# Two buffers for the layer's turned input, and an earlier place for its transposes

## The chip, the cores and the metric

One core of a Trainium2 chip runs the whole program. The metric is the device time of one execution in microseconds (us); lower is better. A kernel's time is the median of its runs.

## The reference, cut to what matters

```
def _attn_ref(q, k, v, beta):            # B=4, H=8, S=768, D=48, float32
    k_n = k / (norm(k) + 1e-06)
    for t in range(S):
        y[:, :, t] = q[:, :, t] @ state
        v_old = state^T k_n[:, :, t]
        state = state + beta_t * outer(k_n[:, :, t], v_t - v_old)

def _moe_ref(x, w_in, w_out):            # 3072 tokens, 384 -> 2048 -> 384
    h = x @ w_in
    sp = log1p(exp(min(h, 20)))  (h itself above 20)
    return (h * tanh(sp)) @ w_out
```

`reference` computes the first, lays its y out as 3072 rows of 384 (token by head and depth), and puts them through the second. The first part is a recurrence over 768 steps for 32 pairs of batch and head; the second is a layer with one weight matrix in and one out.

## The kernel before, in words

The sequence is cut into `NS` = 12 chunks of `C` = 64 steps. For each chunk n the recurrence is turned into matrix products: products of keys, a triangular solve (`early`, one for two chunks, a long chain of VectorE steps in L296 and L301, ended by the transposes of L308 and L317), and the stages `s_a`, `s_b`, `s_gq`, `s_z` and `s_y`, which are small matmuls with a copy by ScalarE or VectorE behind each. `s_y(n, h)` gives the output y of the chunk for half h of the pairs: ScalarE copies it into the tile `yy` (L487), and the state for the next chunk into `xx` (L486).

The layer works on the 256 tokens of a chunk. `transposed(n, y)` turns y (called a turn here): six TensorE transposes (L505) into two PSUM tiles `xt`, two ScalarE casts to the high part of x (L507), two VectorE subtractions to its low part (L508). The transposes of the first 128 tokens need half 0 of y, the others half 1. `g1(fp)`, for 8 units fp of 256 hidden columns each, runs 18 first-layer matmuls (L530) into a PSUM tile `h`, of which there are two, and then the activation: L534 (ScalarE), L535 (VectorE), L536, L537, L538 (ScalarE), L539 (VectorE, which reads `h` last and frees it), L549 (ScalarE), L552 (VectorE). `g2(fp)` runs 12 second-layer matmuls (L564) on the result; it is issued two units behind `g1`.

In which order all this is traced is written down as due times in chunks: `put(gen, count, t0, t1)` files steps of a generator between t0 and t1, and the plan is run in order of those times. With NFP = 8, `g1(fp)` of chunk n is due at n + (fp + 0.25)/8 and a `g2` at n + (fp + 0.75)/8. `s_y(n, 1)`, which completes y of chunk n, is due at n - 0.2 from chunk 3 on (at 0.6 for n = 1, at 1.8 for n = 2); the stage `s_a` of an even chunk just behind it at n - 1.19, and `s_b` with the next `s_a` at n - 1.07 (n even), so both fall to the boundary ahead of an odd chunk. The turn of chunk n (L708 to L710) is due at n - 0.5/8. A solve for two chunks (L737) runs from 2.6 chunks ahead of its even chunk to 1.5 ahead.

A planner with a time model then settles each engine's order from these priorities and from when inputs are ready. On TensorE that freedom ends for what is due at 0.9 (`m0`) or later: its instructions are issued there in the order of the due times (L744 to L748). ScalarE and VectorE keep the planner's order all along. Each engine executes its order as laid down, and each instruction waits for its inputs.

Pools: `mp` has a tile of its own for each tag and buffer; `x0` and `x1` (high and low part of x) have `bufs=1`, so the turn of chunk n writes them after the last `g1` of chunk n - 1 has read them. The PSUM pool `pa` (tag `at`, four buffers) serves `xt` and nearly all matmuls of the stages.

Around a boundary into chunk n, TensorE's order before the change is thus: g1(n-1,6); s_y(n,1); [s_a at odd n]; a g2; g1(n-1,7); [s_b and s_a at odd n]; the turn of n; a g2; g1(n,0).

Of the kernel before, what the change touches and what calls it, by code (L numbers as in the profile page):

```python
# [10 lines left out]
F32R = mybir.dt.float32r  # L11
# [23 lines left out]
def kernel(  # L35
# [32 lines left out]
    P = 128  # L68
# [4 lines left out]
    NCH = DM // P  # L73
    NF = DFF // P
    NFP = NF // 2
    UT = B * C
# [8 lines left out]
    mp = ctx.enter_context(tc.tile_pool(name="mp", bufs=2))  # L85
# [412 lines left out]


    def transposed(n, y):  # L500
        xs = [mp.tile([P, NCH, UT], F32R, tag=f"x{i}", name=f"x{i}_{n}", bufs=1) for i in range(2)]
        for t in range(UT // P):
            ps = pa.tile([P, NCH, P], F32, tag="at", name=f"xt{n}_{t}")
            for c in range(NCH):
                nc.tensor.transpose(ps[:, c, :], y[:, t, c * P:(c + 1) * P], ident)  # L505
            hi = xs[0][:, :, t * P:(t + 1) * P]
            nc.scalar.copy(out=hi, in_=ps)  # L507
            nc.vector.tensor_tensor(out=xs[1][:, :, t * P:(t + 1) * P], in0=ps, in1=hi, op=ALU.subtract)  # L508
        return xs
# [83 lines left out]
    ys, xs = {}, {}  # L593

    def turn(n):
        if n < NS:
            xs[n] = transposed(n, ys[n])

    def one(f, *a):
        f(*a)  # L600
        yield
# [3 lines left out]
    def put(gen, n, t0, t1):  # L605
        plan.extend((t0 + (t1 - t0) * (i + 0.5) / n, len(plan), gen) for i in range(n))
# [72 lines left out]
    for i, p in enumerate(parts):  # L679
        ny = 4 if i >= TN.get('sg', 14) else 3  # L680
        for j in range(ny):
            x = i + (j + 0.5) / ny
            for (t0, i0), (t1, i1) in zip(cuts, cuts[1:]):
                if i0 <= x < i1:
                    t = t0 + (t1 - t0) * (x - i0) / (i1 - i0)
# [8 lines left out]
    t = 0.0  # L694
    lag = 2
    for k, (n, fp) in enumerate(todo1):
        t = n + (fp + 0.25) / NFP
# [3 lines left out]
        elif k >= lag:  # L701
            m, fq = todo2.pop(0)
            t = n + (fp + 0.75) / NFP
# [2 lines left out]
        put(one(units[m][1], fq), 1, NS + i, NS + i)  # L706
    put(merge(1), 4, *TN['m1'])
    for n in range(1, NS):  # L708
        t = n - 0.5 / NFP
        put(one(turn, n), 1, t, t)  # L710

        t = TN['p1'] if n == 1 else TN['p2'] if n == 2 else n - 1.85
        put(one(prep, n), 1, t, t)
# [11 lines left out]
    for g in range(1, NS // 2):  # L725
        n = 2 * g
# [58 lines left out]
```

## Time and profile before

| | |
|---|---|
| median of 3 runs | 746.64 us (746.27 to 752.27) |
| profiled execution, own time | 750.13 us |
| its span, first to last instruction | 748.4 us |
| mean granted TensorE clock, as a share of 2.4 GHz | 0.905 |

The profile is of one execution. Its page gives each engine's busy time and a strip of 40 slices; the trace behind it gives each instruction's start and duration, what its engine waited for, and the clock granted to TensorE in any stretch. The engines are written PE (TensorE), PEld (its weight loads), DVE (VectorE), ACT (ScalarE), POOL (GpSimd) and SP (SyncE). An idle time in brackets behind a row is the time for which that engine stood before the instruction, and behind the arrow is what ended it.

### The profile page before, as it was taken

Reading aid. Unit: us, or ns where it says so; the run is one execution under the profiler, and the core shown is the slowest. Engines: PE = TensorE matmul, PEld = TensorE weight load, DVE = VectorE, ACT = ScalarE, POOL = GpSimd, SP = SyncE. Lnnn points to the kernel's source line nnn. Section 1 sums busy time; section 2 is a strip of 40 time slices with the busy share of each in tenths; the row PEclk is TensorE's granted clock in tenths of the full one; section 3 lists DMA queues with packets and bytes.
Section 4 is the critical chain, followed back from the end, with each engine's and each line's share of the span. In section 5 each row is a group of like instructions: output and inputs, shape, how many; then the busy total and the mean of one; then the engine's idle time right before and its main releaser. Section 6 shows DMA issues by size and latency. Waiting matters only on the chain.

```text
span 748.4 us, 22288 instructions
## 1 busy us (share of the span) xinstructions
PE 638.7 (85%) x9653; PEld 590.4 (79%) x9670; DVE 509.8 (68%) x1011; ACT 432.0 (58%) x793; POOL 136.2 (18%) x171
## 2 busy tenths in 40 slices
PE   5667455793998899898998997998998989999993
PEld 3236344793897799797998997998997989999993
DVE  4788999757459975389963698864799735553441
ACT  2224534563555567565666646675655777776771
POOL 5343243772032224000010010010000100000000
PEclk9757665796999899899999998999999999999997
DMA  5858710110341222122212302311112121000000
GB/s 83 196 173 243 224 24 1 22 24 1 44 80 30 33 55 45 28 50 31 43 36 35 63 14 33 66 30 26 34 24 34 42 33 34 12 9 15 6 18 21
DMA packets 160210, 37.72 MB, mean 50 GB/s; under 512 B 153456, under 2 KB 156528, under 8 KB 160112
## 3 DMA queue, kind: packets, MB, share of 16 engines
q1 hardware_dynamic: 160112, 36.30, 23.7%
q8 instruction: 76, 1.25, 0.7%
q14 instruction: 22, 0.18, 0.1%
HBM read 31.56 MB, written 4.72 MB: 48 GB/s over the span
## 4 chain that ended last, share of the span: by engine, by line
PE 47%; DVE 26%; ACT 8%; POOL 5%; SPq 5%; issue 5%; DMA 3%; DVEq 0%; POOLq 0%; ACTq 0%
PE h L530 20%; PE acc L564 17%; SPq L137 5%; DVE gt L301 5%; DVE pr L296 4%; PE gq L395 3%; DVE e L539 2%; PE py L395 2%; DMA vt<-in_v_dram 1%; DVE e L535 1%; DVE gt L252 1%; POOL gt L301 1%; PE pz L395 1%; ACT e L536 1%; POOL pr L296 1%
## 5 line engine op out<-in xcount | busy, mean ns | idle before, releaser
L530 PE MATMUL h<-x,wi 128*128 128x256 f32 x1728 | 239.1, 294 | 27.8 <-ACT x L507 15.3
L530 PEld LDWEIGHTS h<-x,wi 128*128 128x128 f32 x1728 | 229.6, 200 | 35.1 <-ACT x L507 17.9
L564 PE MATMUL acc<-wo,g 128*128 128x384 f32 x1152 | 222.8, 342 | 0.1
L564 PEld LDWEIGHTS acc<-wo,g 128*128 128x128 f32 x1152 | 198.2, 188 | 3.8 <-issue 0.2
L539 DVE SCALAR_TENSOR_TENSOR e<-e,h 128x512 f32<-128x512 f32 x96 | 65.6, 684 | 89.5 <-ACT e L538 89.0
L536 ACT ACTIVATE e<-e 128x512 f32<-128x512 f32 x96 | 60.6, 631 | 60.7 <-DVE e L535 60.6
L534 ACT ACTIVATE e<-h 128x512 f32<-128x512 f32 x96 | 57.1, 595 | 66.4 <-PE h L530 61.0
L535 DVE TENSOR_SCALAR e<-e 128x512 f32<-128x512 f32 x96 | 44.4, 463 | 69.6 <-ACT e L534 69.5
L549 ACT CAST g<-e 128x512 fp32r<-128x512 f32 x96 | 59.4, 619 | 54.2 <-DVE e L539 53.8
L376 POOL TENSOR_TENSOR vt<-vt,ne 128x384 f32<-128x384 f32 x24 | 21.7, 905 | 238.3 <-DVE ne L286 109.0
L538 ACT ACTIVATE e<-e 128x512 f32<-128x512 f32 x96 | 60.6, 632 | 2.5
L537 ACT ACTIVATE e<-e 128x512 f32<-128x512 f32 x96 | 60.6, 631 | 2.5
L552 DVE TENSOR_TENSOR g<-e,g 128x512 fp32r<-128x512 f32 x72 | 49.8, 692 | 15.6 <-ACT g L549 14.0
L296 DVE TENSOR_TENSOR pr<-gt 128x228 f32<-128x228 f32 (+14 forms) x147 | 55.2, 376 | 5.1 <-POOL gt L301 1.1
L301 DVE TENSOR_TENSOR gt<-gt,pr 128x228 f32<-128x228 f32 (+14 forms) x147 | 52.9, 360 | 3.3
L395 PE MATMUL gq<-xx,kt 64*64 64x112 f32 (+1 forms) x768 | 49.6, 288 | 0.6 <-ACT at L247 0.6
L395 PE MATMUL py<-xx 128*64 128x48 f32 x768 | 43.9, 230 | 7.2 <-ACT xx L464 7.2
L395 PEld LDWEIGHTS py<-xx 128*64 128x64 f32 x768 | 40.1, 143 | 11.6 <-ACT xx L464 8.7
L552 POOL TENSOR_TENSOR g<-e,g 128x512 fp32r<-128x512 f32 x24 | 31.8, 1325 | 75.7 <-ACT g L549 48.9
L395 PEld LDWEIGHTS gq<-xx,kt 64*64 64x64 f32 x768 | 43.7, 156 | 1.5 <-ACT at L247 0.9
L395 PE MATMUL pz<-vt,tt 64*64 64x48 f32 x768 | 40.8, 245 | 3.9 <-DVE vt L443 3.9
L395 PEld LDWEIGHTS pz<-vt,tt 64*64 64x64 f32 x768 | 36.8, 148 | 8.7 <-issue 6.1
(98 smaller groups left out, 782.7 us busy)
## 6 DMA issues: line engine op xcount, KB each, us to landing
ri<-in_moe_w_in_dram SPq DMA_DIRECT2D x12, 512.0 KB
ro<-in_moe_w_out_dram SPq DMA_DIRECT2D x16, 384.0 KB
vt<-in_v_dram SPq DMA_DIRECT2D x48, 96.0 KB
xx<-in_k_dram SPq DMA_DIRECT2D x48, 96.0 KB
out_dram<-o SPq DMA_DIRECT2D x24, 192.0 KB
qsrc<-in_q_dram SPq DMA_DIRECT2D x48, 64.0 KB
ksrc<-in_k_dram SPq DMA_DIRECT2D x44, 64.0 KB
qsrc<-in_q_dram SPq DMA_DIRECT2D x48, 32.0 KB
```

Of the source, the lines that this page charges most:

```text
L296: queue(eng.tensor_tensor(out=pv, in0=nj, in1=xj, op=ALU.mult), on)
L301: queue(eng.tensor_tensor(out=below, in0=below, in1=pv, op=ALU.add), on)
L395: last[:] = [nc.tensor.matmul(*a, start=True, stop=True)]
L530: nc.tensor.matmul(h[:, f2, :], wt["i", f * P // WI * NCH + c][:, i2, f0:f0 + P], x[:, c, :], start=(i == 0), stop=(i == 3 * NCH - 1))
L534: nc.scalar.activation(e, h, AF.Exp)
L536: nc.scalar.activation(e, e, AF.Square)
L537: nc.scalar.activation(e, e, AF.Ln, bias=0.5, scale=0.5)
L538: nc.scalar.activation(e, e, AF.Exp, scale=-1.0)
L539: nc.vector.scalar_tensor_tensor(e, e, -1.0, h, op0=ALU.add, op1=ALU.mult)
L549: nc.scalar.copy(out=gg[:, 0], in_=e)
L552: eng.tensor_tensor(out=gg[:, 1], in0=e, in1=gg[:, 0], op=ALU.subtract)
L564: nc.tensor.matmul(acc[t], gg[:, a, f2, ts_], wt["o", f][:, i2, :], start=(f == 0 and i == 0), stop=(f == NF - 1 and i == 2))
```

## The change

The two parts of x get two buffers each. The turn of chunk n, for n from 1 on, is due at n - 1.1/8: behind the g2 that is due at n - 1.25/8 and ahead of g1(n-1,7), due at n - 0.75/8. For n = 1 that is 0.8625.

```diff
     def transposed(n, y):
-        xs = [mp.tile([P, NCH, UT], F32R, tag=f"x{i}", name=f"x{i}_{n}", bufs=1) for i in range(2)]
+        xs = [mp.tile([P, NCH, UT], F32R, tag=f"x{i}", name=f"x{i}_{n}", bufs=2) for i in range(2)]
...
     for n in range(1, NS):
-        t = n - 0.5 / NFP
+        t = n - 1.1 / NFP
         put(one(turn, n), 1, t, t)
```

## Rows read from the trace of the kernel before

**Rows 1.** The page: busy time of each engine with its share of the span; the granted TensorE clock in 40 slices of the span, in tenths; and the shares of the engines in the chain of work that ended last.
```profile
PE 638.7 (85%) x9653; PEld 590.4 (79%) x9670; DVE 509.8 (68%) x1011; ACT 432.0 (58%) x793; POOL 136.2 (18%) x171
...
PEclk9757665796999899899999998999999999999997
...
PE 47%; DVE 26%; ACT 8%; POOL 5%; SPq 5%; issue 5%; DMA 3%; DVEq 0%; POOLq 0%; ACTq 0%
```

**Rows 2.** Waits of TensorE's matmuls from 190 us to the end: waiter, what it waited for, total us, how often, the longest.
```profile
PE h L530 <- ACT x L507: 15.3, 8, 2.8
PE h L530 <- DVE x L508: 7.3, 7, 2.3
PE h L530 <- DVE e L539: 5.0, 5, 1.8
PE pg L241 <- DVE kt L222: 1.3, 1, 1.3
PE pg L241 <- issue: 1.2, 2, 0.6
```

**Rows 3.** TensorE's timeline, rows of L530 that had to wait: start, duration, instruction and count, idle time ahead of it. First one that lies outside a turn, then those of turns 3, 5 and 9.
```profile
232.52 2.37 PE L530 MATMUL h<-x,wi 128*128 128x256 f32 x18 [0.81 <-DVE e L539]
...
303.05 4.67 PE L530 MATMUL h<-x,wi 128*128 128x256 f32 x18 [2.80 <-ACT x L507]
...
406.98 0.38 PE L530 MATMUL h<-x,wi 128*128 128x256 f32 x1 [2.17 <-ACT x L507]
407.65 3.19 PE L530 MATMUL h<-x,wi 128*128 128x256 f32 x17 [0.29 <-DVE x L508]
...
614.44 0.38 PE L530 MATMUL h<-x,wi 128*128 128x256 f32 x1 [2.14 <-ACT x L507]
615.11 2.28 PE L530 MATMUL h<-x,wi 128*128 128x256 f32 x17 [0.29 <-DVE x L508]
```

**Rows 4.** Stretches behind the stalls of turns 2 (two), 3, 4, 5, 6, 7, 8 and 9: length, busy time and count of each engine, then the mean granted clock as a share of 2.4 GHz, the DMA engines' share and GB/s.
```profile
238.00:246.00 8.00, 6.19 (x35) 5.87 (x34) 7.63 (x16) 6.11 (x11) 1.45 (x1) 0.79 0.24 42
246.00:256.00 10.00, 6.34 (x61) 5.70 (x63) 9.24 (x19) 4.93 (x9) 2.92 (x2) 0.83 0.31 39
302.00:312.00 10.00, 8.86 (x91) 8.20 (x92) 3.91 (x10) 5.06 (x11) 1.27 (x1) 0.66 0.01 3
354.00:363.00 9.00, 7.05 (x89) 6.49 (x90) 7.94 (x21) 5.98 (x12) 0.00 (x0) 0.81 0.17 21
406.00:414.00 8.00, 6.73 (x87) 6.17 (x88) 3.48 (x9) 3.98 (x9) 0.00 (x0) 0.79 0.01 2
458.00:468.00 10.00, 7.81 (x86) 7.25 (x87) 8.01 (x23) 5.76 (x12) 0.00 (x0) 0.66 0.16 21
512.00:520.00 8.00, 7.26 (x90) 6.69 (x91) 4.13 (x10) 4.24 (x9) 0.00 (x0) 0.79 0.01 2
563.00:571.00 8.00, 5.52 (x80) 5.19 (x82) 6.87 (x19) 4.47 (x9) 0.00 (x0) 0.79 0.23 28
612.00:620.00 8.00, 5.57 (x89) 4.79 (x88) 3.48 (x8) 4.87 (x10) 0.00 (x0) 1.00 0.01 3
```

**Rows 5.** Timelines of TensorE and ScalarE at even turns: the second-layer group behind which the turn comes to stand and the copy of y's second half, at turns 2 and 8 (the first and the last of four), and at turn 4 the ScalarE instruction ahead of the copy that waited for VectorE.
```profile
236.61 2.38 PE L564 MATMUL acc<-wo,g 128*128 128x384 f32 x12
243.07 0.46 ACT L487 COPY yy<-py 128x384 f32<-128x384 f32 x1
...
344.72 0.64 ACT L536 ACTIVATE e<-e 128x512 f32<-128x512 f32 x1 [4.57 <-DVE e L535]
...
553.79 2.38 PE L564 MATMUL acc<-wo,g 128*128 128x384 f32 x12
559.39 0.46 ACT L487 COPY yy<-py 128x384 f32<-128x384 f32 x1
```

**Rows 6.** Timelines of ScalarE, TensorE and VectorE at turn 3: the copy of y's second half, the group ahead of the new place, g1(2,7), the turn's transposes, the next second-layer group, the turn's casts and subtractions.
```profile
290.52 0.48 ACT L487 COPY yy<-py 128x384 f32<-128x384 f32 x1 [0.72 <-PE ps L395]
291.60 2.38 PE L564 MATMUL acc<-wo,g 128*128 128x384 f32 x12
293.81 2.30 PE L530 MATMUL h<-x,wi 128*128 128x256 f32 x18
...
297.26 0.87 PE L505 MATMUL xt<-ident,yy 128*128 128x128 f32 x6
297.89 2.36 PE L564 MATMUL acc<-wo,g 128*128 128x384 f32 x12
302.13 0.86 ACT L507 CAST x<-xt 128x384 fp32r<-128x384 f32 x2
302.64 1.02 DVE L508 TENSOR_TENSOR x<-xt,x 128x384 fp32r<-128x384 f32 x2 [2.06 <-ACT x L507]
```

**Rows 7.** Timelines of TensorE and VectorE at turn 1: the wait for the solve, the turn's transposes, its first subtraction, and the wait for the transpose of the next keys.
```profile
181.33 1.92 PE L395 MATMUL ta<-tt,at 32*32 32x32 f32 x64 [10.90 <-DVE tt L308]
...
190.33 0.82 PE L505 MATMUL xt<-ident,yy 128*128 128x128 f32 x6
191.58 0.55 DVE L508 TENSOR_TENSOR x<-xt,x 128x384 fp32r<-128x384 f32 x1
...
194.58 1.99 PE L241 MATMUL pg<-kt 64*32 64x64 f32 x128 [1.32 <-DVE kt L222]
```

## The prediction

> **What bounds the kernel now.** I read the page first: TensorE is busy 85% of the span, VectorE 68%, ScalarE 58%; the chain that ended last runs 47% over TensorE and 26% over VectorE, and the line of the granted clock has dips between the nines [rows 1]. The first quarter is start-up, on which the change bears only in turn 1. So I asked for TensorE's waits from 190 us on. There are five rows, and two of them are this change's subject: the first-layer matmuls `h` wait 15.3 us for the cast of x (L507) and 7.3 us for its low part (L508), 22.6 us of 30.1; 5.0 us are waits for the buffer of `h` that L539 frees, the rest 2.5 us [rows 2]. Outside these TensorE never idles there, so a microsecond taken from a stall comes off the end unless something else is late next.
>
> Then the timeline at each chunk boundary. Turns 2 to 9 stall, 10 and 11 don't. They are of two kinds. At odd turns (3, 5, 7, 9) one wait of 2.14 to 2.80 us for the cast is followed by one of 0.29 us for the low part [rows 3]. At even turns (2, 4, 6, 8) VectorE is full, 7.94 us busy of 9 at turn 4 [rows 4], with the next triangular solve, and what it owes the layer comes late: ScalarE sits 4.57 us for L535 before it can go on, and in its order the copy of y stands behind that [rows 5].
>
> The fourth view is the granted clock. After most of these stalls it is at half, that is 1.2 instead of 2.4 GHz, for some microseconds: 0.66 on average over 302 to 312 us, 0.79 over 406 to 414, 1.00 over 612 to 620, where the stall was about as long [rows 3, 4]. That time is in no list of waits.
>
> **Part by part.** *The two buffers.* They add no instruction. They remove the write-after-read of x, so that a turn may run before the old chunk's last `h` has read x. Without the move TensorE's hand-written order would hide that; with it, this is what lets the transposes go ahead. The six transposes, two casts and two subtractions of a turn are the same as before: 0.87 us of TensorE at turn 3 [rows 6], and no DMA is among them, so SyncE's and GpSimd's queues lose and gain nothing.
>
> *The move.* A turn's transposes are now issued behind the second-layer group ahead of g1(n-1,7), and not behind g1(n-1,7) itself. Until g1(n,0) needs x there are 18 matmuls of 2.30 us and a second-layer group of 2.36 us in between [rows 6], at odd turns s_b and s_a too. Cast and subtraction took 0.86 and 1.02 us [rows 6]. So x is ready if the cast is not held back over some 3 us.
>
> A. Odd turns, stalls. y is there: at turn 3 its copy ends at 290.52 + 0.48 = 291.00, the group before the new place ends at 291.60 + 2.38 = 293.98 [rows 6]. So no wait for y, and the wait for x goes: 2.80 + (2.17 + 0.29) + (2.17 + 0.29) + (2.14 + 0.29) = 10.15 us (turns 3, 5, 7 and 9; turn 7's two rows read as turn 5's do) [rows 3].
>
> B. Odd turns, clock. A window of length L with mean clock c, with TensorE working in it, loses about (1 - c) L: 3.4 + 1.68 + 1.68 + 0 = 6.76 us [rows 4]. With no stall I count all of it as regained. Its ends are 0 and 6.8.
>
> C. Even turns, stalls. The x waits go there too: 22.6 - 10.15 = 12.45 us. But now TensorE meets the transposes before y is copied, and g1(n-1,7) stands queued behind them. The group before them ends at 238.99, 347.13, 450.78 and 556.17; the copy of y at 243.53, 350.26, 454.56 and 559.85 (four turns, the first and the last of them shown) [rows 5]. That makes new waits of 4.54 + 3.13 + 3.78 + 3.68 = 15.13 us. They swallow the waits that g1(n-1,7) had for the buffer of `h`, 5.0 - 0.81 = 4.19 us (the row at 232.52 lies outside a turn) [rows 2, 3]. Net gain 12.45 + 4.19 - 15.13 = 1.51 us. The ends: y's copy at once behind its matmuls, no new wait, a gain of 16.6; one more link as late as the row of 4.57 us at each of the four, a loss of 16.8. I take 1.51, since every instruction that sets when y is copied stands ahead of the changed ones.
>
> D. Even turns, clock. The five windows lose 1.68 + 1.70 + 1.71 + 3.4 + 1.68 = 10.17 us [rows 4], about six dips of 1.7. One undivided stall in place of two or three should leave one dip a turn, 6.8 us: gain 3.4, between -6.8 (ten dips) and 10.2 (none).
>
> For the clock the rows count 16.9 us in nine windows. The Trainium skill, page "TensorE: Matmul & The Clock Gate", section "Part 1: The HAM clock gate (the "warmup" mystery)", says that the ramp costs under 1% of a typical kernel's span and need not be modelled. As an estimate from that page that is under 7.5 us of 748.4, so the trace doesn't bear it out, and by the page B and D together would be smaller than the 10.2 us I count.
>
> E. Turn 1. Its due time falls from 0.9375 to 0.8625, below the 0.9 at which the hand-written order of TensorE begins, so the planner places it. TensorE idles 10.90 us there for the solve's L308, and before the change runs these transposes at 190.33 [rows 7]; in the idle time they are free (0.8 us, and the 1.32 us wait for L222 may shrink). But both subtractions, 0.55 us each [rows 7], then may go into VectorE's solve, which TensorE awaits. Between -1.1 and +2.1; I take 0, as the two are about equal.
>
> F. Turns 10 and 11 have no stall and gain nothing.
>
> G. Giving back. The planner settles ScalarE's and VectorE's orders anew; an order once laid down holds, and a faster TensorE finds some results late. I take one wait as the row of 0.29 us [rows 3] at each of eleven turns, 3.2 us; ends 0 and 7.5 (the waits not for x, 5.0 + 1.3 + 1.2, once over [rows 2]).
>
> Sum: 10.15 + 6.76 + 1.51 + 3.4 + 0 - 3.2 = 18.6 us. The profiled execution took 750.13 us (span 748.4 and 1.7 around it), so 731.5 in its like; it lies 3.5 us above the median of 746.64, which gives 728.0 us.
>
> **Rivals.**
>
> *The clock gives nothing back.* The dips come in other places as often as before. Then 10.15 + 1.51 - 3.2 = 8.5 us, 738.2 us. For it: six dips in four even turns. Against: the windows of turn 9 and the full line from there on show that TensorE keeps 2.4 GHz where it doesn't stand. This is a mechanism of B and D; the page named above, by which the ramp is small, would land nearer here.
>
> *The wait for x stays.* The change doesn't do what it says if ScalarE's order leaves the casts where they are. At turn 3 the transposes end at 298.13 and the cast starts at 302.13 [rows 6], 4 us of other ScalarE work later, and part of that work is fed by matmuls behind g1(n-1,7). Then A, B and C bring nothing, D's 3.4 less the 1.7 of one new dip remains: 745.0 us. Against: the planner places by when an input is ready, and that is earlier by a group and 18 matmuls.
>
> *Slower: TensorE stands behind y.* Place: the four even turns. If y's copy slips one more late link of 4.57 us there, 18.3 us are added, with one more dip each 6.8 us: -16.9 - 1.5 + 18.3 + 6.8 + 3.2 = +9.9, 756.5 us. It is slower than before from 3.0 us of slip a turn ((16.9 + 1.5 - 3.2 - 3.4) / 4, with half of the dips). For it: L535's lateness of 4.57 us is of that size already. Against: the old order has it, and nothing ahead of the copy is moved. The Trainium skill, same page, section "Part 2: What happens when you issue a matmul", says that matmuls stay in program order and only weight loads are pulled ahead; by that the 18 matmuls can't overtake the transposes, which is what this rival needs.
>
> *Better: y is in time.* If the shorter odd turns shift the planner's order so that y is copied right behind its matmuls, C gives 16.6 and D 10.2: 10.15 + 6.76 + 16.6 + 10.2 - 3.2 = 40.5 at most; half of the gap to the forecast gives 717 us. For it: ScalarE is free when y's matmuls end. Against: its order there is set by VectorE's full queue.
>
> **How the numbers follow.** About 1% (7.5 us) is what a measurement of this kernel can tell from no change. Forecast 0.55; clock gives nothing 0.15 (split 0.09 faster, 0.06 same, as it lies at that bound); wait stays 0.12 (0.03, 0.08, 0.01); slower 0.08 (0.02 of it same); y in time 0.10. Faster 0.55 + 0.09 + 0.03 + 0.10 = 0.77, same 0.06 + 0.08 + 0.02 = 0.16, slower 0.01 + 0.06 = 0.07. The forecast's own range is 720 to 737; with the rivals on both sides, 716 to 743.
>
> **What would show it.** Right: `h` waiting for L507 and L508 gone from TensorE's waits, at odd turns no stall and full clock in the windows; at even turns one new wait of the transposes for L487 of 3 to 4.5 us, with g1(n-1,7) right behind it; turn 1's transposes inside the idle time before 181 us. Wrong: casts that still start 4 us behind their transposes (A), dips at odd turns without a stall (B), waits for L487 above 6 us (C), L308 of the solve ahead of turn 1 over 1 us later (E), and new rows of waits for L539 or L464 above 7.5 us together (G).

## The result: 725.21 us, and the profile after

| | before | after |
|---|---|---|
| median | 746.71 us | 725.21 us |
| lowest to highest of 4 runs | 746.27 to 752.27 us | 720.66 to 728.14 us |
| profiled execution (span) | 750.13 us (748.4) | 728.14 us (726.4) |

The ratio of the times is 0.969 (95% interval 0.9619 to 0.9761): 3.1% faster. The two profiled spans differ by 22.0 us.

The page of the changed kernel, TensorE's share, its granted clock in 40 slices, and the chain that ended last, beside [rows 1]:
```profile
PE 627.8 (86%) x9653; PEld 584.9 (81%) x9670; DVE 508.7 (70%) x1011; ACT 431.8 (59%) x793; POOL 136.6 (19%) x171
...
PEclk9879665798799899999999998999999999999997
...
PE 52%; DVE 24%; ACT 7%; SPq 6%; issue 4%; POOL 3%; DMA 3%; DVEq 0%; ACTq 0%; POOLq 0%
```
The work is the same (the same instruction counts), TensorE is busy 10.9 us less, in part since less of it runs at half clock (its mean granted clock is 0.919 and was 0.905), and more of the last chain is TensorE's own.

TensorE's waits in the changed kernel, from 180 us on (columns as in [rows 2], and the wait of [rows 7] with them; two rows of under 1 us left out):
```profile
PE xt L505 <- ACT yy L487: 15.5, 4, 4.3
PE ta L395 <- DVE tt L308: 10.4, 1, 10.4
PE pg L241 <- DVE kt L222: 3.1, 1, 3.1
PE h L530 <- DVE e L539: 1.2, 2, 0.8
...
```
Against [rows 2] the two waits for x, 22.6 us, are gone without a rest. In their place stands one new row: the transposes wait for the copy of y, 15.5 us in four waits. The prediction had 15.13 us in four.

The clock in stretches around turns 2 to 9 of the changed kernel (columns as in [rows 4], which holds the like of before):
```profile
236.00:252.00 16.00, 11.72 (x119) 11.26 (x118) 15.35 (x32) 8.06 (x15) 4.06 (x4) 0.79 0.32 46
292.00:304.00 12.00, 12.00 (x257) 11.51 (x256) 3.91 (x6) 10.16 (x19) 1.57 (x2) 1.00 0.34 49
340.00:354.00 14.00, 10.35 (x108) 9.94 (x110) 12.92 (x32) 9.93 (x19) 0.00 (x0) 0.88 0.28 40
390.00:402.00 12.00, 12.00 (x257) 11.51 (x256) 5.23 (x11) 9.64 (x18) 0.00 (x0) 1.00 0.32 44
438.00:454.00 16.00, 12.54 (x124) 11.98 (x123) 14.26 (x35) 10.79 (x20) 0.00 (x0) 0.79 0.24 33
488.00:500.00 12.00, 12.00 (x258) 11.59 (x256) 4.91 (x10) 9.75 (x19) 0.00 (x0) 1.00 0.37 52
538.00:554.00 16.00, 11.91 (x128) 11.40 (x126) 14.97 (x37) 11.85 (x23) 0.00 (x0) 0.89 0.23 31
586.00:598.00 12.00, 12.00 (x257) 11.51 (x256) 5.43 (x12) 10.24 (x20) 0.00 (x0) 1.00 0.32 45
```
The odd turns (every second line) have TensorE busy 12.00 of 12 us at full clock. The even ones still stand and still dip: (1 - clock) times length is 3.36 + 1.68 + 3.36 + 1.76 = 10.2 us, what the five even stretches of [rows 4] had.

Turn 3 in the changed kernel, timelines of ScalarE, TensorE and VectorE (compare [rows 6]):
```profile
290.24 0.48 ACT L487 COPY yy<-py 128x384 f32<-128x384 f32 x1 [0.51 <-PE ps L395]
291.31 2.38 PE L564 MATMUL acc<-wo,g 128*128 128x384 f32 x12
293.53 0.82 PE L505 MATMUL xt<-ident,yy 128*128 128x128 f32 x6
294.10 2.38 PE L530 MATMUL h<-x,wi 128*128 128x256 f32 x18
...
296.27 0.55 DVE L508 TENSOR_TENSOR x<-xt,x 128x384 fp32r<-128x384 f32 x1
...
299.85 2.30 PE L530 MATMUL h<-x,wi 128*128 128x256 f32 x18
```
The second subtraction ends at 296.82, three microseconds ahead of g1(3,0) at 299.85; that unit takes 2.30 us where it took 4.67 [rows 3].

Turn 4, VectorE, ScalarE and TensorE (compare the ScalarE row at 344.72 in [rows 5]); between the two VectorE rows stand 13 solve steps (L296, L301):
```profile
332.92 0.68 DVE L552 TENSOR_TENSOR g<-e,g 128x512 fp32r<-128x512 f32 x1
...
338.50 0.42 DVE L535 TENSOR_SCALAR e<-e 128x512 f32<-128x512 f32 x1
338.18 2.38 PE L564 MATMUL acc<-wo,g 128*128 128x384 f32 x12
338.95 0.63 ACT L536 ACTIVATE e<-e 128x512 f32<-128x512 f32 x1 [4.56 <-DVE e L535]
340.40 0.49 PE L505 MATMUL xt<-ident,yy 128*128 128x128 f32 x3
344.02 0.46 ACT L487 COPY yy<-py 128x384 f32<-128x384 f32 x1
344.54 0.55 PE L505 MATMUL xt<-ident,yy 128*128 128x128 f32 x3 [3.65 <-ACT yy L487]
344.84 3.64 PE L530 MATMUL h<-x,wi 128*128 128x256 f32 x18
```
The first half's transposes go at once; the second half's wait 3.65 us for y, because ScalarE waited 4.56 us for L535 (4.57 before) and has six more instructions in its order before the copy of y; and the 18 matmuls behind them then run at half clock for a while, 3.64 us and not 2.30. The Trainium skill, page "TensorE: Matmul & The Clock Gate", section "Part 2: What happens when you issue a matmul", says that matmuls keep their program order; the trace agrees, these 18 had their inputs and start 0.30 us behind the first late transpose.

Turn 1, TensorE and VectorE (compare [rows 7]), and in the last row VectorE's L222 in the kernel before, where L539 follows it at 194.36:
```profile
183.64 1.54 PE L505 MATMUL xt<-ident,yy 128*128 128x128 f32 x6
193.23 0.69 DVE L539 SCALAR_TENSOR_TENSOR e<-e,h 128x512 f32<-128x512 f32 x1 [2.02 <-ACT e L538]
193.83 1.24 DVE L222 STREAM_TRANSPOSE kt<-ksrc 128x1024 f32<-128x1024 f32 x1
195.22 3.60 PE L241 MATMUL pg<-kt 64*32 64x64 f32 x128 [3.06 <-DVE kt L222]
...
193.20 1.24 DVE L222 STREAM_TRANSPOSE kt<-ksrc 128x1024 f32<-128x1024 f32 x1
```
The planner put the transposes behind the idle time, not into it, and set L222 behind L539. Before, L222 stood ahead of it; TensorE's wait for it is 3.06 us, not 1.32, and behind it the clock is at half for a while (0.57 on average over 195 to 199 us), so that the same 128 matmuls take 3.60 us and not 1.99.

Where the 22.0 us are, by the end of each chunk's first unit (last matmul of g1(n,0), from TensorE's timelines of both):

| chunk n | before, us | after, us | gained since the chunk before |
|---|---|---|---|
| 0 | 126.7 | 127.4 | -0.7 |
| 1 | 199.0 | 201.1 | -1.4 |
| 2 | 255.3 | 254.4 | 3.0 |
| 3 | 307.7 | 302.2 | 4.6 |
| 4 | 359.4 | 353.0 | 0.9 |
| 5 | 410.8 | 399.8 | 4.6 |
| 6 | 464.6 | 451.6 | 2.0 |
| 7 | 516.0 | 498.5 | 4.5 |
| 8 | 569.6 | 550.9 | 1.2 |
| 9 | 617.4 | 595.8 | 2.9 |
| end | 748.4 | 726.4 | 0.4 |

The four odd turns give 16.6 us, the four even ones 7.1, turn 1 costs 1.4. Another 0.7 was lost ahead of chunk 0's first unit, whose end lies between 125.2 and 128.9 us in the profiles here. (A dip that reaches past a row's mark counts in the next row, up to 1 us each.)

### The profile page after: what moved, and what is told of

Same layout as the page of the kernel before. It is cut to its first block, busy times and chain, and to the rows that moved or that the text cites. A ratio compares the mean times of both kernels' runs of the same rounds, so it can differ in the third digit from the quotient of the medians.

```text
span 726.4 us, 22302 instructions
## 1 busy us (share of the span) xinstructions
PE 627.8 (86%) x9653; PEld 584.9 (81%) x9670; DVE 508.7 (70%) x1011; ACT 431.8 (59%) x793; POOL 136.6 (19%) x171
## 3 DMA queue, kind: packets, MB, share of 16 engines
q8 instruction: 76, 1.25, 0.7%
## 4 chain that ended last, share of the span: by engine, by line
PE 52%; DVE 24%; ACT 7%; SPq 6%; issue 4%; POOL 3%; DMA 3%; DVEq 0%; ACTq 0%; POOLq 0%
PE h L530 21%; PE acc L564 20%; SPq L137 6%; DVE pr L296 3%; DVE gt L301 3%; PE gq L395 3%; PE py L395 2%; DVE e L539 2%; ACT e L537 1%; DMA vt<-in_v_dram 1%; DVE mo L193 1%; DVE gt L252 1%; ACT e L536 1%; PE ta L395 1%; DVE xx L446 1%
## 5 line engine op out<-in xcount | busy, mean ns | idle before, releaser
L530 PE MATMUL h<-x,wi 128*128 128x256 f32 x1728 | 232.0, 290 | 1.2 <-DVE e L539 1.2
L530 PEld LDWEIGHTS h<-x,wi 128*128 128x128 f32 x1728 | 225.0, 196 | 3.0 <-issue 1.3
L564 PE MATMUL acc<-wo,g 128*128 128x384 f32 x1152 | 223.5, 343 | 0.6 <-issue 0.6
L564 PEld LDWEIGHTS acc<-wo,g 128*128 128x128 f32 x1152 | 199.6, 189 | 4.7 <-issue 1.0
L539 DVE SCALAR_TENSOR_TENSOR e<-e,h 128x512 f32<-128x512 f32 x96 | 65.8, 685 | 90.3 <-ACT e L538 89.6
L535 DVE TENSOR_SCALAR e<-e 128x512 f32<-128x512 f32 x96 | 44.2, 461 | 48.6 <-ACT e L534 48.3
L552 DVE TENSOR_TENSOR g<-e,g 128x512 fp32r<-128x512 f32 x72 | 50.5, 701 | 20.2 <-ACT g L549 18.5
L538 ACT ACTIVATE e<-e 128x512 f32<-128x512 f32 x96 | 60.6, 632 | 2.5
L296 DVE TENSOR_TENSOR pr<-gt 128x228 f32<-128x228 f32 (+14 forms) x147 | 54.5, 371 | 4.2 <-PE warm L298 0.5
L301 DVE TENSOR_TENSOR gt<-gt,pr 128x228 f32<-128x228 f32 (+14 forms) x147 | 52.2, 355 | 3.6
L395 PE MATMUL py<-xx 128*64 128x48 f32 x768 | 45.6, 233 | 8.8 <-ACT xx L464 8.6
L552 POOL TENSOR_TENSOR g<-e,g 128x512 fp32r<-128x512 f32 x24 | 31.7, 1321 | 79.3 <-ACT g L549 60.0
L395 PE MATMUL gq<-xx,kt 64*64 64x112 f32 (+1 forms) x768 | 44.6, 267 | 1.6 <-DVE xx L446 1.0
L395 PE MATMUL ps<-xx 128*48 128x48 f32 x704 | 41.1, 216 | 0.0
L395 PEld LDWEIGHTS gq<-xx,kt 64*64 64x64 f32 x768 | 38.8, 140 | 2.6 <-PE gq L395 1.1
L446 DVE TENSOR_TENSOR xx<-gq,amask 64x256 f32<-64x256 f32 x96 | 40.1, 418 | 0.8
```

The costliest lines, as they stand in the source:

```text
L296: queue(eng.tensor_tensor(out=pv, in0=nj, in1=xj, op=ALU.mult), on)
L301: queue(eng.tensor_tensor(out=below, in0=below, in1=pv, op=ALU.add), on)
L395: last[:] = [nc.tensor.matmul(*a, start=True, stop=True)]
L530: nc.tensor.matmul(h[:, f2, :], wt["i", f * P // WI * NCH + c][:, i2, f0:f0 + P], x[:, c, :], start=(i == 0), stop=(i == 3 * NCH - 1))
L538: nc.scalar.activation(e, e, AF.Exp, scale=-1.0)
L539: nc.vector.scalar_tensor_tensor(e, e, -1.0, h, op0=ALU.add, op1=ALU.mult)
```

## The experiments

My theory was the prediction's: the gain is the wait for x and the clock behind it; at odd turns both go, at even turns a wait for y replaces it, because ScalarE's copy of y stands behind an L535 that is late on VectorE. Rivals: the second buffer alone does it; the planner's new orders do it by luck; VectorE's queue sets the pace at even turns wherever TensorE's wait shows. Where kernels ran on different chips, they are compared by their ratios to the kernel before on the same chip.

**Two buffers alone.**
```diff
-        t = n - 1.1 / NFP
+        t = n - 0.5 / NFP
```


> Two buffers for x, the turn at its old place. The order of instructions on every engine is that of the kernel before. My theory (the gain comes from where the transposes stand): no gain, 745 to 749 us, and the waits of h for L507 and L508 stay at about 22.6 us. Rival (the buffer itself frees the casts, since they no longer wait for the last h of the old chunk): the waits shrink and it is 5 to 20 us faster.

746.58 us, ratio 1.0003 (0.9966 to 1.004). The waits of `h` for L507 and L508 are 16.5 and 7.5 us. So the buffers alone do nothing.

**The move alone.**
```diff
-        xs = [mp.tile(..., tag=f"x{i}", name=f"x{i}_{n}", bufs=2) for i in range(2)]
+        xs = [mp.tile(..., tag=f"x{i}", name=f"x{i}_{n}", bufs=1) for i in range(2)]
```


> The turn at its new place, x with one buffer, so the casts still have to wait until g1(n-1,7) has read the old x. My theory: at odd turns g1(n-1,7) is followed by s_b, s_a and a second-layer group, 3.6 us, and casts and subtractions need 1.9 us, so much of the gain comes without the second buffer: 728 to 738 us, with short waits for L507 or L508 at even turns. Rival (the second buffer is what carries it): 742 to 750 us, with the waits for L507 and L508 as before.

734.2 us, ratio 0.9839 (0.9788 to 0.989): about half of the gain. Its TensorE waits from 200 us on:
```profile
PE xt L505 <- ACT yy L487: 17.6, 4, 7.0
...
PE h L530 <- DVE x L508: 1.1, 1, 1.1
```
The time is in the expected range, but not for the reason I gave alone: the waits for x are nearly gone even so (1.1 us), and what is worse than in the changed kernel is a wait for y of 7.0 us at turn 4. There VectorE's order came out otherwise, and L535 was 5.87 us late. The second buffer's worth lies partly in the orders that the planner makes of it; how much of the difference is the buffer by itself stays open there. At odd turns it adds nothing: from the end of one chunk's first unit to the next, turns 3, 5, 7 and 9 take 46.9, 46.8, 46.8 and 44.9 us with one buffer, and 47.8, 46.8, 46.8 and 44.9 in the changed kernel. The move alone loses 5.5 us to it at turn 4, where the clock behind the 7.0 us is 0.57 over 346 to 358 us (0.88 in the changed kernel).

**Odd turns alone.**
```diff
-        t = n - 1.1 / NFP
+        t = n - (1.1 if n % 2 and n > 1 else 0.5) / NFP
```


> Two buffers; only turns 3, 5, 7, 9 and 11 move, turns 1, 2, 4, 6, 8 and 10 stay. My theory: the odd turns carry 16 to 17 us, the even ones 7 and turn 1 loses 2, so 730 us (728 to 733), no stall and no dip of the clock at odd turns, all as before at even ones. Rival (at the even turns the wait for y takes all that the wait for x gave): as fast as the changed kernel or faster, 722 to 726 us. Second rival (the gain is a lucky new order of ScalarE and VectorE, not the wait): over 738 us.

730.33 us, ratio 0.9795 (0.9741 to 0.9849). Over 292 to 304, 388 to 400, 488 to 500 and 586 to 598 us, its odd turns, TensorE is busy 12.00 of 12 us at a clock of 1.00. Of `h` there remain 6.4 us of waits for L508, 4.8 for L507, four each, the even turns', and 6.7 for L539. The place of the transposes carries the odd turns' gain; the even turns are worth less, as the theory had it.

**Turn 1 back.**
```diff
-        t = n - 1.1 / NFP
+        t = n - (0.5 if n == 1 else 1.1) / NFP
```


> The changed kernel with turn 1 alone back at its old due time. My theory: turn 1 costs 2 us in the changed kernel, since the planner puts the key transpose L222 behind L539 there, so this takes 723 us (722 to 724 in the median, if the spread lets it be seen), and TensorE's wait for L222 is 1.3 us again in place of 3.1. Rival (the 2 us come from the clock's stretches in the start-up, which differ from run to run): the wait shrinks and the end of chunk 1's first unit stays where it is.

728.94 us, ratio 0.978 (0.9732 to 0.9828): no faster than the changed kernel, a miss in the time. At turn 1 it went as expected: the wait for L222 is 1.3 us and chunk 1's first unit ends at 199.4 and not 201.1. It was lost at turn 6 (TensorE's timeline) and, by 1.3 us, at turn 8:
```profile
436.35 0.49 PE L505 MATMUL xt<-ident,yy 128*128 128x128 f32 x3
442.75 0.90 PE L505 MATMUL xt<-ident,yy 128*128 128x128 f32 x3 [5.91 <-ACT yy L487]
```
In VectorE's order there 15 solve steps (L296, L301) stand between the L552 and the L535 in question, and 13 in the changed kernel, where that wait was 3.46 us. Of the 2.45 us more, 0.72 is the copy of y being later (442.24 and not 441.52 us); the rest is TensorE being there 1.73 us earlier (the second-layer group ahead of the turn starts at 434.14 and not 435.87). So an edit at turn 1 moved an order five chunks on, and what TensorE had gained it spent waiting for the same copy. This is the prediction's slower rival on a small scale, and it pointed to VectorE's order as what to test.

**Filling the stand at even turns.**
```diff
             ps = pa.tile([P, NCH, P], F32, tag="at", name=f"xt{n}_{t}")
+            for _ in range(30 if t == 1 and n in (2, 4, 6, 8) else 0):
+                nc.tensor.matmul(ps[:, 0:2, :].rearrange("p a b -> p (a b)"), ident.bitcast(BF16)[:, 0:P], ident.bitcast(BF16), start=True, stop=True)
```


> The changed kernel with 30 extra matmuls of 256 columns (bf16, of the identity, into the PSUM tile that the transposes then overwrite) ahead of the second half's transposes at turns 2, 4, 6 and 8, where TensorE stands 3.5 to 4.3 us for y. At 0.107 us each, if streamed at full clock, they take 3.2 us of a time in which it would stand. My theory: the stretches at half clock that follow these stalls come from the standing; they go, and 8.6 us of time lost at half clock with them: 715 to 719 us. Rival (the clock at even turns falls whatever TensorE does there, or the filler costs as much as it gives): 724 us or more.

727.86 us, ratio 0.975 (0.9711 to 0.979), beside 0.968 for the changed kernel on the same chip: not faster, and outside the expected 715 to 719 us. At three of the four turns the clock stood as the theory said. Stretches around turns 4, 6 and 8 (columns as above; TensorE's busy time holds the filler):
```profile
340.00:354.00 14.00, 12.00 (x92) 11.08 (x91) 13.46 (x34) 8.03 (x16) 0.00 (x0) 1.00 0.30 42
440.00:454.00 14.00, 12.61 (x150) 11.75 (x148) 13.46 (x35) 8.06 (x16) 0.00 (x0) 1.00 0.25 35
538.00:554.00 16.00, 14.24 (x157) 13.12 (x155) 15.35 (x43) 9.59 (x19) 0.00 (x0) 1.00 0.24 34
```
All three are at 1.00, where the changed kernel had 0.88, 0.79 and 0.89 in such stretches (its second profile, below, has 1.00 at two of them without a filler, so this alone doesn't show what the filler does). At turn 2, which had the filler too, TensorE then stood 3.53 us for the second subtraction and the clock fell behind that (0.91 over 240 to 254 us). And the time was not regained. Turn 4, TensorE (the lines stand two lower, L530 is L532 and L508 L510):
```profile
341.81 3.44 PE L505 MATMUL xt<-ident 128*128 128x256 bf16 x30
345.66 0.55 PE L507 MATMUL xt<-ident,yy 128*128 128x128 f32 x3 [0.41 <-ACT yy L487]
345.96 2.38 PE L532 MATMUL h<-x,wi 128*128 128x256 f32 x18
...
352.16 2.30 PE L532 MATMUL h<-x,wi 128*128 128x256 f32 x17 [1.60 <-DVE x L510]
```
The 18 matmuls take 2.38 us in place of 3.64, and then TensorE waits for the second subtraction, which stands behind solve steps on a VectorE that is busy 13.46 of 14 us: 8.0 us of such waits at four turns. With the stand filled, TensorE meets VectorE at the next place.

**Even turns in two halves.**
```diff
+        if n in (2, 4, 6, 8):
+            put(one(turn, n, 0), 1, n - 1.1 / NFP, n - 1.1 / NFP)
+            put(one(turn, n, 1), 1, n - 0.5 / NFP, n - 0.5 / NFP)
...                                 # turn(n, half) does one half of the tokens
```


> The changed kernel, but at turns 2, 4, 6 and 8 only the first half's transposes stand at the new place; the second half's stay at the old one, behind g1(n-1,7). My theory: the wait for y (15.5 us at four turns) goes, the wait for the second half's cast and low part comes in its place with 1 to 3 us a turn, since only one second-layer group of 2.4 us lies between: 718 to 724 us. Rival (at even turns VectorE's full queue sets the pace, whichever wait shows it): 724 to 728 us, with the sum of stalls at these turns as in the changed kernel.

730.05 us, ratio 0.9771 (0.9736 to 0.9806), slower than the changed kernel and above both expected ranges. TensorE's waits from 200 us on (L508 is L513 here, L507 L512, L505 L510, L530 L535, L539 L544):
```profile
PE h L535 <- DVE x L513: 7.0, 4, 2.5
PE h L535 <- DVE e L544: 6.0, 7, 1.5
PE h L535 <- ACT x L512: 5.8, 4, 2.3
PE xt L510 <- ACT yy L487: 1.6, 4, 0.4
```
The wait for y is 1.6 us, as planned, and the sum of the stands is 20.4 where it was 16.7. That fits the rival, by which VectorE's queue sets the pace at even turns and moving TensorE's work only renames the wait; what tests it is a change of VectorE's order, below.

**The changed kernel again.** The same text, run on the chip of the two above and the one below.

> The changed kernel once more, on the chip of these runs, to compare the others with: 722 to 728 us by every theory.

722.77 us, ratio 0.968 (0.9642 to 0.9718). In this profile the clock is 1.00 around turns 4 and 6, with the same waits for y (14.9 us). (1 - clock) times length over the four even turns is 3.4 us here, 10.2 in the first profile; the spans are 722.1 and 726.4. So the dips behind the same stalls differ between these two runs by 6.8 us, and the spans by 4.3.

**Solve steps kept behind L535.**
```diff
+    def behind(ins, g):
+        done = [m for t, m in es if t + 0.4 / 8 <= now[0]]
+        if g > 1 and done:
+            order(ins, done[-1])
+        return ins
...
-            queue(eng.tensor_tensor(out=pv, in0=nj, in1=xj, op=ALU.mult), on)
+            queue(behind(eng.tensor_tensor(out=pv, in0=nj, in1=xj, op=ALU.mult), g), on)
...                                 # the same at L301; es holds due time and L535 of each unit,
...                                 # now[0] the due time of what is being issued
```


> The changed kernel with one more order on VectorE: a step of the solve (from the second pair of chunks on) that is due 0.05 chunks or more behind a unit's g1 stands behind that unit's L535. At turn 4 six solve steps, no longer fourteen, then stand between L552 and the L535 on which ScalarE and the copy of y wait. My theory: y is late at even turns because of these eight steps of 0.4 us (3.2 us); the transposes' wait for L487 falls from 15.5 us to under 5, most of the stretches at half clock at even turns go, and the kernel takes 705 to 714 us. Rival (the solve becomes late instead): L487 is on time but TensorE waits for L308 or L317 at s_a and s_b, 722 us or more. Second rival (y is late for another reason): nothing moves, 724 to 727 us.

706.75 us, ratio 0.9454 (0.9417 to 0.9492), beside 0.968: the best version, as predicted in size. (The lines stand eight lower: L487 is L495, L505 L513, L530 L538, L535 L543, L564 L572.) TensorE's waits from 200 us on:
```profile
PE xt L513 <- ACT yy L495: 3.4, 3, 2.2
...
PE h L538 <- DVE e L547: 0.5, 1, 0.5
...
```
and turn 4, VectorE (L552 is L560, L535 L543; six solve steps between them), TensorE and ScalarE:
```profile
329.33 0.69 DVE L560 TENSOR_TENSOR g<-e,g 128x512 fp32r<-128x512 f32 x1
...
332.02 0.42 DVE L543 TENSOR_SCALAR e<-e 128x512 f32<-128x512 f32 x1
...
334.42 2.38 PE L572 MATMUL acc<-wo,g 128*128 128x384 f32 x12
336.63 0.49 PE L513 MATMUL xt<-ident,yy 128*128 128x128 f32 x3
337.44 0.46 ACT L495 COPY yy<-py 128x384 f32<-128x384 f32 x1
337.96 0.55 PE L513 MATMUL xt<-ident,yy 128*128 128x128 f32 x3 [0.83 <-ACT yy L495]
```
The wait for y at turn 4 is 0.83 us where it was 3.65. The solve is not late for it: no wait for its results appears. (The expectation counted fourteen steps before; the trace has thirteen, and six now.)

**The same with more steps ahead.**
```diff
-        done = [m for t, m in es if t + 0.4 / 8 <= now[0]]
+        done = [m for t, m in es if t + 0.9 / 8 <= now[0]]
```


> As the kernel with solve steps kept behind L535, but only steps due 0.11 chunks or more behind the unit's g1 (0.9 in place of 0.4 units): nine solve steps and not six stand ahead of the L535 in question at turn 4, and fourteen without the order. My theory (y is late by what these steps take, 0.4 us each): the transposes wait about 1.2 us a turn longer for L487, 7 to 10 us in all in place of 3.4, and the kernel takes 709 to 715 us, between 706.75 and the changed kernel. Rival (any such order does it, its size is of no account): 705 to 708 us.

714.51 us, ratio 0.9546 (0.9496 to 0.9597), between the two; the wait for y is 7.6 us in four, and at turn 4 1.88 us with nine steps ahead. Six, nine and thirteen steps go with 0.83, 1.88 and 3.65 us: 0.35 to 0.44 us a step, what a step takes. That is shown, then, for turn 4: y is late there by the solve steps that stand ahead of L535. Turn 6 bears it out, where the same counts go with no wait, 0.96 and 3.46 us. At turn 8 the count alone does not give the wait: 4, 3 and 8 steps go with 0.27, 1.78 and 4.09 us. At turn 2, where the wait fell from 4.28 to 2.94 and 2.25 us, no L552 of VectorE stands near to count from. So the place of the solve steps is shown as the cause at turns 4, 6 and 8 and for about half of the wait at turn 2; that the count gives its size is shown at two turns.

**The kernel before, with that order.**
```diff
-        xs = [mp.tile(..., tag=f"x{i}", name=f"x{i}_{n}", bufs=2) for i in range(2)]
+        xs = [mp.tile(..., tag=f"x{i}", name=f"x{i}_{n}", bufs=1) for i in range(2)]
...
-        t = n - 1.1 / NFP
+        t = n - 0.5 / NFP
```


> The kernel before (one buffer for x, the turn at its old place) with the order on VectorE that keeps solve steps behind L535. It tells what the change is worth where VectorE's order no longer sets the pace at even turns. My theory: x is still waited for at all turns from 2 to 9, 2.5 us each, with dips of the clock behind; against the changed kernel with the same order (706.75 us) that is 20 to 29 us more, so 727 to 736 us, and the change is worth about as much at even turns as at odd ones. Rival (the order on VectorE was the fault all along, the place of the turn matters little): 707 to 720 us.

728.27 us, ratio 0.973 (0.9673 to 0.9788). The size is as expected; the place is not. Its waits of `h` from 200 us on (L507 is L515, L508 L516):
```profile
PE h L538 <- ACT x L515: 14.2, 5, 3.9
PE h L538 <- DVE x L516: 2.9, 5, 1.3
```
are at turns 2, 3, 5, 7 and 9 and not at eight turns (turn 4 has one of 0.8 us). Between the ends of chunk 3's and 4's first units it takes 47.2 us, and 46.5 with the change; 46.5 and 45.7 from 5 to 6, 46.9 and 46.6 from 7 to 8; but 50.2 and 46.8 from 4 to 5, 51.3 and 46.9 from 6 to 7. So at turns 4, 6 and 8 the place of the transposes is worth under 1 us once VectorE's order is right; at turn 2 it is worth 1.5, and at odd turns 3.4 to 5.7 us with that order and 2.9 to 4.6 without.

**That order, and turn 1 back.**
```diff
-        t = n - 1.1 / NFP
+        t = n - (0.5 if n == 1 else 1.1) / NFP
```


> The changed kernel with the order on VectorE and turn 1 alone at its old due time. My theory: TensorE's wait for L222 is 1.3 us and not 3.1, the first unit of chunk 1 ends 1.5 to 2 us earlier, and as y is no longer late at even turns this comes through to the end: 704 to 706 us. Rival (the planner's order elsewhere moves by more than that, as it did with this edit alone): 707 us or more.

708.17 us (705.78 to 709.6), ratio 0.9467 (0.9421 to 0.9513): not to be told from 0.9454. The wait for L222 is 1.3 us again; whether it reaches the end is unclear.

## Why the prediction was right

The median came out 2.8 us below the forecast of 728.0, inside the forecast's own range.

*A and B, odd turns, 16.9 us: right, and shown.* 16.6 us by the ends of the units; no wait for x, no dip; and the odd turns alone give their part without the others. That the second buffer is what lets the transposes go ahead was wrong there: with one buffer the odd turns took the same time.

*C, even turns' stalls, +1.5 us: right.* The waits that went were 16.6 us, the new ones 15.5 (predicted 15.1). The assumption that what sets the copy of y isn't touched held at turns 2 and 4, where ScalarE waited 4.36 and 4.56 us for L535 (4.36 and 4.57 before). At turns 6 and 8 the order changed: 13 and 8 solve steps stood ahead of L535 and not 16, and ScalarE waited 5.20 and 2.93 us (5.91 and 5.82 before). That the new waits there, 3.46 and 4.09 us, still came near the predicted 3.78 and 3.68 was luck in part. It does not hold in general either: the move alone and turn 1's edit alone changed VectorE's order and made one such wait 7.0 and 5.91 us. The slower rival had its place and its mechanism right, and its size was there at one turn, not at four.

*D, even turns' clock, +3.4 us: wrong in size.* In the profiled run it is 10.2 us before and after, so 0. The second profile of the same kernel has 3.4, a gain of 6.8. One dip a turn was a guess at something that varies between runs.

*E, turn 1, 0: wrong, -1.4 us*, outside its bounds of -1.1 to 2.1 (-2.1 with the 0.7 lost ahead of it). I had priced the two subtractions in VectorE's solve. They went behind it, and the transposes behind the idle time, at 183.64 us and not before 181; what I had not priced is that the planner re-sorts L222, which made TensorE's wait 1.74 us longer, as putting turn 1 back shows, and the dip of the clock behind that. Over 192 to 204 us the clock is 0.86 in six of the seven profiles with turn 1 moved and 1.00 in the six with it at its old place. In the seventh (even turns in two halves) the wait is 3.2 us, the clock 1.00, and chunk 1's first unit ends 70.9 us behind chunk 0's, where the changed kernel takes 73.7 and the kernel before 72.4; how the loss is shared between wait and clock stays open.

*G, giving back, -3.2 us: wrong in sign.* No wait for L539 or L464 came up; 1.2 us of waits for L539 remain of 5.0. With A to E as measured (E with the 0.7), 10.15 + 6.76 + 1.1 + 0 - 2.1 = 15.9 us, and the spans differ by 22.0: 6.1 us more was gained than the waits and the windows name. Part of it can be read from turn 9, where no dip disturbs: the waits there were 2.14 + 0.29 = 2.43 us [rows 3], and the chunk gained 2.9. Each stop costs some 0.2 us beside the wait shown, as the first matmul behind it takes 0.38 us by itself where 18 in a row take 2.30; 4 stops at turns 2 to 9 in place of 19 make about 3 us. This is argued from rows; no run measured it alone. The remaining 3 us stay open. Part of the half-clock time of the changed kernel falls while TensorE stands anyway and costs nothing (at turn 2 the clock is 0.50 over 243.1 to 245.4 us, where no matmul runs), and two profiles of this kernel differ by more than that (4.3 us).

So 18.6 stood against 22.0 us in the profiled spans: D and E were too high by 5.5 us together, G too low by 9.3, and they partly cancelled, which was luck; A, B and C, where the argument lay, were right to 1 us.

*The rivals.* "The wait for x stays" is refuted: 22.6 us went to nothing. "The clock gives nothing back" is refuted for odd turns, and true of the even ones in the profiled run. The Trainium skill, page "TensorE: Matmul & The Clock Gate", section "Part 1: The HAM clock gate (the "warmup" mystery)", puts the ramp penalty under 1% of a typical kernel's span. That is said of the slow matmuls at the start of a kernel. The prediction held it against the 16.9 us of 748.4 (2.3%) that the trace of before had at boundaries in mid-kernel, which are another thing, so these rows neither bear that sentence out nor refute it. "Better: y is in time" was worked out at 40.5 us at most, 706.1 us; once VectorE's order was mended the kernel took 706.75. That the two agree so closely is luck, as 3.4 us of waits for y were left and E and G came out otherwise.

## What to carry to other kernels

When a producer is moved ahead on an in-order engine, list which of its inputs is late at the new place: the wait for x became a wait for y wherever y was late, and the cure for that was on another engine's queue. Where a chain of small steps shares a queue with work that others wait for, count the steps ahead of the waited-for instruction; each was worth its 0.4 us at turn 4, and ordering them gave another 16.0 us (722.77 to 706.75) where the change had given 22.8 on that chip. Judge an edit under an automatic planner by the orders it gives everywhere, since what was gained in one chunk was lost five chunks on.

## What the runs showed of the hardware

Behind the same stalls the clock dipped in one execution and not in the next: four even turns lost 10.2 and 3.4 us at half clock in two profiles of one kernel, with waits for y of 15.5 and 14.9 us. With thirty filler matmuls in the stand the clock was 1.00 at turns 4, 6 and 8, in one profile, and fell at turn 2 behind another stand of 3.53 us. That the standing is what lets it fall fits all the profiles here, but one without a filler had 1.00 at two of these turns too, so it is not shown.
